# Low parts of the weights by accumulating transfers, and unread matmuls in the first gather

## The chip, the cores and the metric

The kernel runs on one core of a Trainium2 chip. The metric is the device time of one execution in microseconds (us). The engines are TensorE (PE in the profile, its weight loads PEld), VectorE (DVE), ScalarE (ACT), GpSimd (POOL) and SyncE (SP). SP issues plain transfers; POOL issues gathers, scatters and, after the change, accumulating transfers, which go through one software queue (q0).

## The reference

Three layers follow one another on 3072 tokens of 384 values (8 heads of 48):

```python
for t in range(S):                       # linear attention, 768 steps, 4 x 8 heads
    cur = einsum('bhd,bhe->bhde', u[None] * kt, vt)
    y[:, :, t] = einsum('bhd,bhde->bhe', rt, state + cur)
    state = wt[:, :, :, None] * state + einsum('bhd,bhe->bhde', kt, vt)
...
expert_idx = argmax(xn @ en.T / tau)     # first layer of 8 experts: one expert per token
out[mask] = gate_w * (relu(x[mask] @ w1[e]) @ w2[e])
...
order = argsort(-logits.flatten())       # second layer: greedy, 384 tokens per expert
for idx in order: ...                    # take (token, expert) if both are still free
out[mask] = relu(x[mask] @ w1[e]) @ w2[e]
```

w1 is 384 x 1024 and w2 is 1024 x 384 for each of the 8 experts of both layers, all in float32.

## The kernel before, in words

The kernel computes float32 products from two parts of each operand. `hi` is the value rounded to the matmul's format (fp32r), `lo` is what is left, and `prod3` (L548 to L550) adds hi x hi, hi x lo and lo x hi. So every weight is split once: it lands in a tile `stage` (three buffers of 128x1536, 768 KB, half of a weight matrix), ScalarE copies it into `whi`, and the low part `wlo = stage - whi` is computed by another engine. `whi` and `wlo` have three buffers each (`wpool`).

The attention (0 to about 225 us) runs in 24 chunks. A step begins on VectorE with the scan L295. VectorE makes the scaled r, k and masked products, TensorE transposes and multiplies, ScalarE copies transposes out of PSUM (kT L322, xT L389) and makes `cv` (L341). After steps 4, 8, 12 and so on the tokens of the steps done are given to experts (`choose`) and POOL scatters them to the expert's rows (L442). Beside this the first three weight matrices of the first expert layer are loaded (`early`, by `wparts`), their low part on POOL (L196); from the fourth step on, each step takes one piece.

The first expert layer (to about 512 us) is not touched by the change; its weights go through `wload`, low parts on VectorE.

The second expert layer (to 844 us) has eight phases, one expert each, with w1 products (`pH`), relu and split into h2h (ScalarE, L544) and h2l (VectorE, L545), and w2 products (`pY`). Which expert is next, and which 384 tokens it takes, is found by `chain(p)`: a search in which VectorE writes comparison tables (`cmp`, L972), TensorE counts with them (L983, L990, L994) and VectorE reads the counts; it gives `ei`, the expert's number. `compact` turns the chosen tokens into row numbers `ix` with one-hot matmuls (L1107, L1111), and POOL gathers the rows (L1124, three transfers of 128 rows). `tin` transposes them (pX, L1164). `load2(p, i)` fetches the two weight matrices of phase p once `ei` is known and splits them: ScalarE `whi` L1149, VectorE `wlo` L1150, in four pieces of 128x384 per half, so 16 pieces per phase. The chain, the gather and the loads of phase p+1 run during phase p. In the last two phases no search is left.

The order of the work on each engine is fixed ahead of the run by a scheduler that simulates the program with priorities; `issue_after` ties an operation behind another. Each engine then works through its list and waits at its head.

Of the kernel before, what the change touches and what calls it, by code (L numbers as in the profile page):

```python
# [26 lines left out]
DM = H * D  # L27
N = B * S
E = 8
# [15 lines left out]
WST = 3  # L45
TB = 2
# [29 lines left out]
WNQ = 2  # L76
# [7 lines left out]
def tile_kernel(ctx: ExitStack, tc, rd, kd, wd, vd, ud, emb, tau, m1w1, m1w2, m1w2t, wg2, m2w1, m2w2, out):  # L84
# [99 lines left out]
    def wparts(i, e, nq=2, eng=None):  # L184
        hi = wpool.tile([128, FW], F32R, name="whi")
        lo = wpool.tile([128, FW], F32R, name="wlo")
        WT[i, e] = (hi, lo)
        h = FW // 2
        for q in range(2):
            t = stg.tile([128, h], F32, name="stage")  # L190
            nc.sync.dma_start(t, M1[i][e][:, q * h:(q + 1) * h])
            g = h // nq
            for o in range(0, h, g):
                s = slice(q * h + o, q * h + o + g)
                nc.scalar.copy(hi[:, s], t[:, o:o + g])  # L195
                (eng or nc.vector).tensor_tensor(lo[:, s], t[:, o:o + g], hi[:, s].bitcast(F32), op=ALU.subtract)  # L196
                yield
# [45 lines left out]
    with tc.tile_pool(name="ld", bufs=3) as ld, tc.tile_pool(name="wk", bufs=2) as wk, \  # L243
# [220 lines left out]
        early = (x for i, e in ((0, 0), (1, 0), (0, 1)) for x in wparts(i, e, WNQ, nc.gpsimd))  # L464
# [6 lines left out]
        for st in range(NST):  # L471
# [23 lines left out]
            if st > WST:  # L495
                next(early, None)
# [417 lines left out]
    with tc.tile_pool(name="m2", bufs=2) as mp, tc.tile_pool(name="ps2", bufs=2, space=PSUM) as ps:  # L914
# [9 lines left out]
        oqi = [None]  # L924
        pcm = ps.tile([128, 512], F32, name="pcm", bufs=1)

        def chain(p):
# [4 lines left out]
            if not last:  # L932
# [30 lines left out]
                for s in range(3):  # L963
                    for lv in range(2):
# [17 lines left out]
                        for a in range(J // 2):  # L982
                            nc.tensor.matmul(px, cmp[:, 2 * KS * a:2 * KS * a + 128],  # L983
                                             oh[:, 2 * a:2 * a + 2, :].rearrange("p b e -> p (b e)"),
                                             start=(a == 0), stop=(a == J // 2 - 1))
                        xs = small([128, 2, E], "xs", FP16)
                        nc.vector.tensor_tensor(xs, px.rearrange("p (b e) -> p b e", b=2), par16, op=ALU.mult)
                        pa = pcn[:, o:o + 8]
                        for b in range(2):
                            nc.tensor.matmul(pa[:, :E], psum2, xs[:, b], start=(b == 0), stop=(b == 1))  # L990
# [3 lines left out]
                        nc.tensor.matmul(pb[:, :E], ones[:KS, :], fl, start=True, stop=True)  # L994
# [134 lines left out]
        def load2(p, i):  # L1129
# [7 lines left out]
            for q in range(2):  # L1137
# [7 lines left out]
                pieces = LP0 if p == 0 else LP  # L1145
                g = h // len(pieces)
                for r, e in enumerate(pieces):
                    c = slice(q * h + r * g, q * h + r * g + g)
                    nc.scalar.copy(hi[:, c], t[:, r * g:r * g + g])  # L1149
                    (nc.vector if e == "v" else nc.gpsimd).tensor_tensor(lo[:, c], t[:, r * g:r * g + g], hi[:, c].bitcast(F32),  # L1150
                                                                         op=ALU.subtract)
# [126 lines left out]
```

## Time and profile before

| | |
|---|---|
| Median of 3 runs | 845.6 us (840.58 to 848.67) |
| Profiled execution | 846.28 us, span 844.4 us, mean granted TensorE clock 0.933 |
| Busy share of the span | PE 91%, DVE 66%, ACT 40%, POOL 20% |
| PE in the chain that ended last | 53% of the span |
| q1 (plain transfers) | 87.71 MB, 32.0% of the 16 DMA engines' span |
| q0 (POOL's transfers) | 18.98 MB, 6.3% |

A line of the trace names an instruction by its line in the kernel, its engine, the operation and the tiles it writes and reads. "Idle before" is the time its engine stood still before it, with what ended that. A granted clock of 1.00 is TensorE's level of 2.4 GHz, 0.5 would be the level of 1.2 GHz all the time. Shares of busy time are averages over stages with different limits, so the stages are read apart.

### The profile page before, as it was taken

How to read it: one execution, taken by the hardware profiler on the slowest of the kernel's cores; microseconds unless marked ns; L12 is line 12 of the kernel's file. 1: busy time of each engine (PE TensorE's matmuls, PEld its weight loads, DVE VectorE, ACT ScalarE, POOL GpSimd, SP SyncE). 2: the span in 40 equal slices, each digit the busy share in tenths (PEclk: the TensorE clock that was granted, in tenths of full speed). 3: DMA queues.
4: the chain of work that ended last, by engine and by line, in shares of the span. 5: the costliest groups of instructions: out<-in, count | busy, mean ns of one | idle time of the engine just before them, and what ended most of it. 6: DMA issues, size and time to landing. Idle time of an engine off the chain costs nothing.

```text
span 844.4 us, 14670 instructions
## 1 busy us (share of the span) xinstructions
PE 771.9 (91%) x5373; PEld 675.0 (80%) x5373; DVE 556.1 (66%) x1719; ACT 335.5 (40%) x851; POOL 168.0 (20%) x173
## 2 busy tenths in 40 slices
PE   5998979999889998899999999697979889899997
PEld 4877768888389897898989888485868778789997
DVE  9998999998425435333644556676878788786430
ACT  3544645556324444334543411333323323335431
POOL 3014540121200320303032002302021221222011
PEclk9997889999979999999999999797969879899999
DMA  8775664540343353333433002332323243426300
GB/s 279 232 247 198 227 219 147 179 142 19 126 144 114 127 167 112 110 106 105 152 123 105 5 1 103 133 111 77 132 75 133 80 155 94 150 68 235 110 29 29
DMA packets 39302, 107.64 MB, mean 127 GB/s; under 512 B 6667, under 2 KB 16701, under 8 KB 39229
## 3 DMA queue, kind: packets, MB, share of 16 engines
q1 hardware_dynamic: 32060, 87.71, 32.0%
q0 software_dynamic: 7168, 18.98, 6.3%
q8 instruction: 43, 0.70, 0.4%
q14 instruction: 31, 0.25, 0.1%
HBM read 87.16 MB, written 19.90 MB: 127 GB/s over the span
## 4 chain that ended last, share of the span: by engine, by line
PE 53%; issue 9%; DVE 4%; POOL 2%; another core or an unknown queue 1%; ACT 1%; DMA 1%; ACTq 0%; POOLq 0%; DVEq 0%
PE pH L548 8%; PE pY L550 7%; PE pY L548 7%; PE pH L549 7%; PE pH L550 7%; PE pY L549 7%; PE pO L687 2%; PE pX L654 2%; PE pcm L1111 1%; PE pcn L983 1%; DVE wlo L1150 1%; POOL x L1124 1%; POOL out_dram L1193 1%; PE pX L1164 1%
## 5 line engine op out<-in xcount | busy, mean ns | idle before, releaser
L548 PE MATMUL pH<-xhi,whi 128*128 128x416 f32 x192 | 73.8, 385 | 11.7 <-DVE hl L545 7.5
L545 DVE SCALAR_TENSOR_TENSOR hl<-pH,hh 128x416 fp32r<-128x416 f32 x64 | 37.6, 590 | 70.6 <-ACT hh L544 60.2
L1150 DVE TENSOR_TENSOR wlo<-stage,whi 128x384 fp32r<-128x384 f32 x128 | 68.3, 550 | 7.0 <-ACT whi L1149 6.8
L548 PE MATMUL pH<-x2h,whi 128*128 128x384 f32 x192 | 70.9, 370 | 1.8 <-DVE h2l L545 1.6
L549 PE MATMUL pH<-x2l,whi 128*128 128x384 f32 x192 | 70.8, 369 | 0.0
L1149 ACT CAST whi<-stage 128x384 fp32r<-128x384 f32 x128 | 57.1, 511 | 33.8 <-PE pH L549 20.2
L550 PE MATMUL pH<-xhi,wlo 128*128 128x416 f32 x192 | 70.3, 367 | 0.0
L549 PE MATMUL pH<-xlo,whi 128*128 128x416 f32 x192 | 70.2, 366 | 0.0
L550 PE MATMUL pH<-x2h,wlo 128*128 128x384 f32 x192 | 69.7, 363 | 0.0
L544 ACT ACTIVATE h2h<-pH 128x384 fp32r<-128x384 f32 x64 | 31.4, 491 | 91.8 <-PE pH L550 90.8
L550 PE MATMUL pY<-whi,h2l 128*128 128x384 f32 x192 | 67.6, 355 | 0.0
L548 PE MATMUL pY<-whi,h2h 128*128 128x384 f32 x192 | 67.4, 351 | 0.0
L549 PE MATMUL pY<-wlo,h2h 128*128 128x384 f32 x192 | 66.8, 349 | 0.0
L195 ACT CAST whi<-stage 128x512 fp32r<-128x512 f32 (+1 forms) x90 | 51.7, 647 | 33.6 <-PE pY L549 23.0
L196 DVE TENSOR_TENSOR wlo<-stage,whi 128x512 fp32r<-128x512 f32 x78 | 48.3, 686 | 25.1 <-ACT whi L195 25.1
L550 PE MATMUL pY<-hh,wlo 128*128 128x416 f32 x168 | 60.4, 360 | 0.0
L548 PE MATMUL pY<-hh,whi 128*128 128x416 f32 x168 | 60.1, 358 | 0.0
L764 POOL DMA_INDIRECT lg<-lr,ids x24 | 23.1, 961 | 185.9 <-DVE lr L689 180.7
L549 PE MATMUL pY<-hl,whi 128*128 128x416 f32 x168 | 59.1, 352 | 0.0
L544 ACT ACTIVATE hh<-pH 128x416 fp32r<-128x416 f32 x64 | 32.8, 515 | 62.5 <-PE pH L550 48.5
L362 PE MATMUL y<-vv,am 128*128 128x48 f32 x384 | 56.3, 276 | 0.0
L1193 POOL DMA_INDIRECT out_dram<-orow,ix x24 | 24.4, 1015 | 156.4 <-ACT orow L1192 141.7
(327 smaller groups left out, 1904.7 us busy)
## 6 DMA issues: line engine op xcount, KB each, us to landing
stage<-in_m1w_dram SPq DMA_DIRECT2D x32, 768.0 KB
stage<-in_m2w_dram SPq DMA_DIRECT2D x32, 768.0 KB
wz<-in_w_dram SPq DMA_DIRECT2D x24, 260.0 KB
rd<-in_r_dram SPq DMA_DIRECT2D x24, 256.0 KB
kd<-in_k_dram SPq DMA_DIRECT2D x24, 256.0 KB
xg<-zt SPq DMA_DIRECT2D x8, 627.2 KB
xr<-xg SPq DMA_DIRECT2D x24, 193.0 KB
vv<-in_v_dram SPq DMA_DIRECT2D x24, 192.0 KB
```

The source lines that it names most:

```text
L195: nc.scalar.copy(hi[:, s], t[:, o:o + g])
L196: (eng or nc.vector).tensor_tensor(lo[:, s], t[:, o:o + g], hi[:, s].bitcast(F32), op=ALU.subtract)
L362: yi = nc.tensor.matmul(y[:, o:o + D], ams[h][:, p, :], vv[:, 2 * p + h, :], start=(c == 0), stop=(c == 0 or h == 1))
L544: nc.scalar.activation(hi, pH, AF.Relu)
L545: nc.vector.scalar_tensor_tensor(lo, pH, 0.0, hi.bitcast(F32), op0=ALU.max, op1=ALU.subtract)
L548: nc.tensor.matmul(o, wh, xh, start=start, stop=False)
L549: nc.tensor.matmul(o, wh, xl, start=False, stop=False)
L550: pe[0] = nc.tensor.matmul(o, wl, xh, start=False, stop=stop)
L764: s = nc.gpsimd.indirect_dma_start(out=dst, out_offset=bass.IndirectOffsetOnAxis(ap=d["ids"][:m, a:a + 1], axis=0), in_=src, in_offset=Non ...
L1149: nc.scalar.copy(hi[:, c], t[:, r * g:r * g + g])
L1150: (nc.vector if e == "v" else nc.gpsimd).tensor_tensor(lo[:, c], t[:, r * g:r * g + g], hi[:, c].bitcast(F32), op=ALU.subtract)
L1193: s_ = nc.gpsimd.indirect_dma_start(out=out, out_offset=bass.IndirectOffsetOnAxis(ap=d["ix"][:, a:a + 1], axis=0), in_=orow, in_offset=None)
```

## The change

- `ADD` names phases 1 to 5 of the second expert layer. For their weights ScalarE writes `whi` and then `-hi` into `wlo` (a scaled copy of the stage into the rounded format), piece by piece; when a half is done, POOL issues one transfer of 768 KB from `stage` that is added to `wlo` in place. The VectorE subtract stays for phases 0, 6 and 7.
- The early weights of the first layer take the same way, in pieces of 128x384 (`WNQ` 4 in place of 2, two pieces per step), in place of the subtract on POOL.
- `warm` adds 42 matmuls of 128x384 with bf16 operands into a `pY` tile that nobody reads, behind the matmuls of the first rounds of `chain(1)`; `HW` has their numbers.

```diff
--- before.py
+++ after.py
@@ -43,6 +43,8 @@
 FP16 = mybir.dt.float16
 SPLIT = 4096.0
 WST = 3
+HW = ((2, 6), (2, 24), (8,))
+ADD = (1, 2, 3, 4, 5)
 TB = 2
 LP0 = "vvvv"
 LP = "vvvv"
@@ -73,7 +75,7 @@
 IT = 1
 OQ = 4
 NSC = 2
-WNQ = 2
+WNQ = 4
 GROUPS = (4, 4, 4, 4, 4, 2, 1, 1)
 GS = max(GROUPS)
 HA = 2
@@ -181,7 +183,7 @@
     M1 = (m1w1, m1w2)
     FW = KT * FF
 
-    def wparts(i, e, nq=2, eng=None):
+    def wparts(i, e, nq=2, add=False):
         hi = wpool.tile([128, FW], F32R, name="whi")
         lo = wpool.tile([128, FW], F32R, name="wlo")
         WT[i, e] = (hi, lo)
@@ -193,7 +195,12 @@
             for o in range(0, h, g):
                 s = slice(q * h + o, q * h + o + g)
                 nc.scalar.copy(hi[:, s], t[:, o:o + g])
-                (eng or nc.vector).tensor_tensor(lo[:, s], t[:, o:o + g], hi[:, s].bitcast(F32), op=ALU.subtract)
+                if add:
+                    nc.scalar.activation(lo[:, s], t[:, o:o + g], AF.Copy, scale=-1.0)
+                    if o + g == h:
+                        nc.gpsimd.dma_start(lo[:, q * h:(q + 1) * h], t.bitcast(F32R), accum_op=ALU.add)
+                else:
+                    nc.vector.tensor_tensor(lo[:, s], t[:, o:o + g], hi[:, s].bitcast(F32), op=ALU.subtract)
                 yield
 
     def wload(i, e, nq=WQ):
@@ -461,7 +468,7 @@
         s2(1)
         s3(0)
         route_consts()
-        early = (x for i, e in ((0, 0), (1, 0), (0, 1)) for x in wparts(i, e, WNQ, nc.gpsimd))
+        early = (x for i, e in ((0, 0), (1, 0), (0, 1)) for x in wparts(i, e, WNQ, True))
         ends, chosen, slot_of = {}, [], {}
         for n in GROUPS:
             s0 = len(slot_of)
@@ -493,7 +500,8 @@
                 if st > 1 and tables:
                     table()
             if st > WST:
-                next(early, None)
+                for _ in range(2):
+                    next(early, None)
             if st == WF:
                 wfold(E - DEF)
             if st > E:
@@ -922,6 +930,14 @@
 
         plan = {}
         oqi = [None]
+        hq = []
+
+        def warm(i, n):
+            if not hq:
+                hq.append(ps.tile([128, DM], F32, name="pY"))
+            with tc.issue_after(i.ins):
+                for _ in range(n):
+                    nc.tensor.matmul(hq[0], ones, ioq.rearrange("p s j -> p (s j)")[:, :DM], start=True, stop=True)
         pcm = ps.tile([128, 512], F32, name="pcm", bufs=1)
 
         def chain(p):
@@ -980,18 +996,24 @@
                         o = 16 * lv
                         px = pcn[:, 48 + o:64 + o]
                         for a in range(J // 2):
-                            nc.tensor.matmul(px, cmp[:, 2 * KS * a:2 * KS * a + 128],
+                            wi = nc.tensor.matmul(px, cmp[:, 2 * KS * a:2 * KS * a + 128],
                                              oh[:, 2 * a:2 * a + 2, :].rearrange("p b e -> p (b e)"),
                                              start=(a == 0), stop=(a == J // 2 - 1))
+                        if p == 1 and s == 1 and lv == 0:
+                            warm(wi, HW[2][0])
                         xs = small([128, 2, E], "xs", FP16)
                         nc.vector.tensor_tensor(xs, px.rearrange("p (b e) -> p b e", b=2), par16, op=ALU.mult)
                         pa = pcn[:, o:o + 8]
                         for b in range(2):
-                            nc.tensor.matmul(pa[:, :E], psum2, xs[:, b], start=(b == 0), stop=(b == 1))
+                            wi = nc.tensor.matmul(pa[:, :E], psum2, xs[:, b], start=(b == 0), stop=(b == 1))
+                        if p == 1 and s == 0:
+                            warm(wi, HW[lv][0])
                         fl = small([KS, E], "fl", BF16)
                         nc.vector.tensor_tensor(fl, pa[:KS, :E], need[:KS], op=ALU.is_ge)
                         pb = pcn[:, o + 8:o + 16]
-                        nc.tensor.matmul(pb[:, :E], ones[:KS, :], fl, start=True, stop=True)
+                        wi = nc.tensor.matmul(pb[:, :E], ones[:KS, :], fl, start=True, stop=True)
+                        if p == 1 and s == 0:
+                            warm(wi, HW[lv][1])
                         nn = small([128, 1], "nn", bufs=4)
                         nc.vector.reduce_max(nn, pb[:, :E], axis=AX.X)
                         if lv == 0:
@@ -1143,12 +1165,17 @@
                                       mybir.DependencyInfo(mybir.DependencyClass.Sync, mybir.DependencyReason.DATA),
                                       reason="rows before weights")
                 pieces = LP0 if p == 0 else LP
+                add = p in ADD
                 g = h // len(pieces)
                 for r, e in enumerate(pieces):
                     c = slice(q * h + r * g, q * h + r * g + g)
                     nc.scalar.copy(hi[:, c], t[:, r * g:r * g + g])
-                    (nc.vector if e == "v" else nc.gpsimd).tensor_tensor(lo[:, c], t[:, r * g:r * g + g], hi[:, c].bitcast(F32),
-                                                                         op=ALU.subtract)
+                    if add:
+                        nc.scalar.activation(lo[:, c], t[:, r * g:r * g + g], AF.Copy, scale=-1.0)
+                    else:
+                        nc.vector.tensor_tensor(lo[:, c], t[:, r * g:r * g + g], hi[:, c].bitcast(F32), op=ALU.subtract)
+                if add:
+                    nc.gpsimd.dma_start(lo[:, sl], t.bitcast(F32R), accum_op=ALU.add)
             d["w", i] = (hi, lo)
 
         sc_o = []
```

The order on the engines moves at more than the places of the diff. Line numbers below are those of each kernel: L1150 before is L1176 after, L1149 is L1172, L545 is L553, L1107 is L1129, L1116 is L1138, L972 is L988, L1124 is L1146, L1193 is L1220.

VectorE in the second phase (p = 1), behind the one-hot tables of the next phase's tokens, before the change:

```order
L1107 TENSOR_TENSOR oq<-ioq,pb_6925 128x128x6
L992 TENSOR_TENSOR fl<-pcn,need 46x8
L1150 TENSOR_TENSOR wlo<-stage,whi 128x384
L996 TENSOR_REDUCE nn<-pcn 128x1
L1114 COPY cp<-pcm 128x15
L1005 TENSOR_SCALAR t_7317<-nn,t_7293 128x1
L1116 SCALAR_TENSOR_TENSOR ix<-cp 128x3
L1118 TENSOR_REDUCE gg<-cp 128x3
L1007 TENSOR_SCALAR wc<-big,t_7317 128x24
L1150 TENSOR_TENSOR wlo<-stage,whi 128x384
L1009 TENSOR_SCALAR w<-wc 128x24
```

and with it:

```order
L1129 TENSOR_TENSOR oq<-ioq,pb_7002 128x128x6
L1012 TENSOR_TENSOR fl<-pcn,need 46x8
L1018 TENSOR_REDUCE nn<-pcn 128x1
L1136 COPY cp<-pcm 128x15
L1027 TENSOR_SCALAR t_7398<-nn,t_7374 128x1
L1138 SCALAR_TENSOR_TENSOR ix<-cp 128x3
L1140 TENSOR_REDUCE gg<-cp 128x3
L1029 TENSOR_SCALAR wc<-big,t_7398 128x24
L553 SCALAR_TENSOR_TENSOR h2l<-pH,h2h 128x384
L1031 TENSOR_SCALAR w<-wc 128x24
```

The subtracts between the steps of the search are gone, and h2l stands where one of them stood.

ScalarE in the first phase (p = 0), at its last relu, before the change:

```order
L540 CAST x2h<-pX 128x384 x3
L544 ACTIVATE h2h<-pH 128x384 x8
L1149 CAST whi<-stage 128x384 x12
L1192 ACTIVATE orow<-pY,gg 128x384
L540 CAST x2h<-pX 128x384 x2
```

and with it, with the tiles' numbers (the w1 halves of p = 1 are stage_6522 and stage_6533, h2h_6596 is the eighth relu of p = 0):

```order
L552 ACTIVATE h2h_6582<-pH_6572 128x384
L1172 CAST whi_6520<-stage_6522 128x384
L1174 ACTIVATE wlo_6521<-stage_6522 128x384
...
L1172 CAST whi_6520<-stage_6533 128x384
L1174 ACTIVATE wlo_6521<-stage_6533 128x384
...
L552 ACTIVATE h2h_6596<-pH_6586 128x384
```

Eight copies and eight negated copies now stand between the seventh and the eighth relu; before, all eight relus came first.

POOL from the first phase's scatters to the gather of p = 2 (x_6966 before, x_7043 after), before the change:

```order
L1124 DMA x_6008<-y_67,ix 128x384 x3
L1124 DMA x_6406<-y_67,ix 128x384 x3
L1193 DMA out_dram<-orow,ix 3072x384 x3
L1124 DMA x_6966<-y_67,ix 128x384 x3
L1193 DMA out_dram<-orow,ix 3072x384 x3
```

and with it:

```order
L1178 DMA wlo<-stage 128x1536
L1146 DMA x_6479<-y_67,ix 128x384 x3
L1178 DMA wlo<-stage 128x1536
L1220 DMA out_dram<-orow,ix 3072x384
L1178 DMA wlo<-stage 128x1536
L1220 DMA out_dram<-orow,ix 3072x384
L1178 DMA wlo<-stage 128x1536
L1220 DMA out_dram<-orow,ix 3072x384
L1178 DMA wlo<-stage 128x1536 x2
L1146 DMA x_7043<-y_67,ix 128x384 x3
```

Each gather but the first has one or two accumulating transfers right ahead of it in POOL's list and on the same queue.

## Rows read from the trace of the kernel before

**Rows 1.** Windows of the attention: length, busy us (and count) per engine, PEclk, DMA share, GB/s.

```profile
45.90:122.60 76.70, 66.21 (x535) 55.88 (x531) 69.60 (x129) 39.07 (x123) 32.86 (x20) 0.80 0.65 216
122.60:196.80 74.20, 72.49 (x712) 61.59 (x714) 73.58 (x173) 39.68 (x143) 8.47 (x8) 1.00 0.48 148
```

**Rows 2.** Timeline of DVE, L295 (start us, us, operation, count).

```profile
45.86 1.23 DVE L295 TENSOR_TENSOR_SCAN PI<-wz,ind 128x516 f32<-128x516 f32 x1
...
122.62 1.22 DVE L295 TENSOR_TENSOR_SCAN PI<-wz,ind 128x516 f32<-128x516 f32 x1
...
196.81 1.23 DVE L295 TENSOR_TENSOR_SCAN PI<-wz,ind 128x516 f32<-128x516 f32 x1
```

**Rows 3.** Groups of DVE, 50 to 125 us: busy us, mean ns, idle before and releasers.

```profile
L310 DVE SCALAR_TENSOR_TENSOR z<-rd,ut,kd 128x128 f32<-128x128 f32 x27 | 19.5, 736 | 0.0
```

**Rows 4.** The same group of DVE, 130 to 205 us.

```profile
L310 DVE SCALAR_TENSOR_TENSOR z<-rd,ut,kd 128x128 f32<-128x128 f32 x40 | 13.1, 337 | 0.0
```

**Rows 5.** Waits of DVE, 45 to 125 us: total us, times, longest.

```profile
DVE tm L369 <- PE KV L275: 5.0, 2, 3.8
```

**Rows 6.** Groups of POOL, 40 to 130 us.

```profile
L196 POOL TENSOR_TENSOR wlo<-stage,whi 128x768 fp32r<-128x768 f32 x12 | 23.4, 1969 | 71.9 <-ACT whi L195 71.9
```

**Rows 7.** Groups of ACT, 50 to 125 us.

```profile
L195 ACT CAST whi<-stage 128x768 fp32r<-128x768 f32 x11 | 8.7, 829 | 1.6 <-DMA stage<-in_m1w_dram 1.6
```

**Rows 8.** A window before the early weights are split.

```profile
20.00:40.00 20.00, 20.00 (x195) 16.90 (x195) 19.67 (x48) 10.38 (x38) 0.00 (x0) 1.00 0.76 230
```

**Rows 9.** Timeline of PE at the first gather (in brackets idle before, releaser).

```profile
543.03 0.66 PE L1164 MATMUL pX<-ident,x 128*128 128x128 f32 x2 [4.53 <-DMA x<-y,ix]
545.31 0.48 PE L1164 MATMUL pX<-ident,x 128*128 128x128 f32 x1 [1.62 <-DMA x<-y,ix]
...
549.66 0.52 PE L548 MATMUL pH<-x2h,whi 128*128 128x384 f32 x1
549.99 0.52 PE L549 MATMUL pH<-x2l,whi 128*128 128x384 f32 x1
```

**Rows 10.** Windows of the second expert layer's phases, columns as in Rows 1.

```profile
552.50:763.20 210.70, 189.93 (x1431) 164.94 (x1431) 163.82 (x709) 69.42 (x154) 39.38 (x33) 0.89 0.32 110
763.20:816.10 52.90, 52.90 (x308) 51.72 (x307) 27.92 (x57) 25.35 (x57) 8.94 (x9) 1.00 0.41 138
```

**Rows 11.** Groups of PE, L549: 552 to 763 us, then 763 to 816.

```profile
L549 PE MATMUL pH<-x2l,whi 128*128 128x384 f32 x120 | 46.0, 384 | 0.0
...
L549 PE MATMUL pY<-wlo,h2h 128*128 128x384 f32 x120 | 42.6, 358 | 0.0
...
L549 PE MATMUL pH<-x2l,whi 128*128 128x384 f32 x48 | 16.1, 336 | 0.0
```

**Rows 12.** Waits of PE, 540 to 845 us: total us, times, longest.

```profile
PE pX L1164 <- DMA x<-y,ix: 11.5, 4, 4.6
PE pcn L983 <- DVE cmp L972: 8.7, 4, 2.5
...
PE pH L548 <- DVE h2l L545: 1.6, 2, 1.5
```

**Rows 13.** Timelines of ACT and DVE in the second phase.

```profile
606.96 0.49 ACT L544 ACTIVATE h2h<-pH 128x384 fp32r<-128x384 f32 x1 [1.55 <-PE pH L550]
...
620.66 0.54 DVE L545 SCALAR_TENSOR_TENSOR h2l<-pH,h2h 128x384 fp32r<-128x384 f32 x1
```

**Rows 14.** Timelines of POOL and PE at the gather of the next phase.

```profile
577.28 1.09 POOL L1124 DMA_INDIRECT x<-y,ix  x1 [32.86 <-DVE gg L1118]
...
580.35 2.14 POOL L1124 DMA_INDIRECT x<-y,ix  x1 [0.30 <-issue]
...
584.57 0.69 PE L1164 MATMUL pX<-ident,x 128*128 128x128 f32 x2 [0.71 <-DMA x<-y,ix]
```

**Rows 15.** DMA, 600 to 625 us: GB/s in 40 equal slices.

```profile
GB/s 0 0 0 0 0 0 0 157 88 364 413 403 442 423 416 413 442 220 20 0 0 0 0 0 26 0 0 0 0 59 147 315 403 391 381 229 194 84 0 0
```

**Rows 16.** Groups of ACT, 552 to 763 us.

```profile
L1149 ACT CAST whi<-stage 128x384 fp32r<-128x384 f32 x83 | 37.1, 511 | 26.5 <-PE pH L549 18.4 <-DMA stage<-in_m2w_dram 7.9
```

## The prediction, made before the changed kernel ran

> **What bounds the kernel now.** I read the windows first, because the share of busy time changes from stage to stage, then the groups of instructions of one engine in one stretch, then the waits of TensorE, and last the timelines at the places the change touches.
>
> In the attention VectorE is the bound: it is busy 69.60 of 76.70 us while the early weights are split and 73.58 of 74.20 us after that [rows 1]. A step is counted from one L295 scan to the next. Seven steps take 45.86 to 122.62 us, 76.8 us; the next ten take 122.62 to 196.81, 74.2 us, or 7.42 each [rows 2]. Both stretches hold the expert choice about every fourth step, so seven steps at 7.42 would be 51.9 us: the early stretch has 24.8 us too many. They lie on VectorE itself: L310 has a mean of 736 ns against 337 later [rows 3, 4]; 27 x 0.40 is 10.8 us in this one line. L369 waits 5.0 us more, for KV from TensorE [rows 5]. The twelve POOL subtracts of 1.97 us, 23.4 us in all, are the only work of the stretch that is missing later [rows 6]: a VectorE operation that meets one lasts until it ends.
>
> In the second expert layer TensorE is the bound, but not evenly. From 552.5 to 763.2 us, five phases with a selection search beside the matmuls, it is busy 189.93 of 210.70 us at a granted clock of 0.89; from 763.2 on, phases without the search, 52.90 of 52.90 at 1.00 [rows 10]. So the five phases contain 20.8 us of idle time and slow matmuls on top: L549 has means of 384 ns (pH) and 358 (pY) there against 336 [rows 11]. Six groups of 120 weight matmuls, on average 35 ns slower, with two overlapping at any time, are 720 x 0.035 / 2, about 12 us. The waits name the releasers: 8.7 us for the comparison tables of VectorE (cmp), 1.6 for h2l, and 11.5 for the gathered rows, of which the first two of 4.5 and 1.6 belong to the first gather [rows 9, 12]. VectorE is late because its order is fixed and the low parts of the weights stand ahead: in the second phase ScalarE had h2h at 606.96, VectorE reached its h2l at 620.66 [rows 13].
>
> **Attention.** Removed: 12 POOL subtracts. With them go the stretched VectorE operations; of the 24.8 us nothing else explains more than noise, so the ceiling is 25 us. Added on ScalarE: 24 copies and 24 negated copies of 128x384 at 0.51 [rows 16] for 12 copies at 0.83 [rows 7]: 24.5 - 10.0 = 14.5 us. ScalarE was busy 39.07 of 76.70 us [rows 1], so it holds them, but they stand in its order between the copies that TensorE waits for (kT, xT, cv); about half, 7 us, I charge as delay. Added on the DMA: six accumulating transfers of 768 KB. The DMA engines were at 0.65 over 76.7 us, 49.9 us of work [rows 1]; six transfers add 11 to 58 us by the bounds below, and 49.9 + 11 is already more than 51.9. Part is prefetch that may slip, part are loads that steps need, and ScalarE waits in order for the stages. Without any early weights steps ran at a share of 0.76 [rows 8], so there is little room. I charge 7 us more. Attention: 25 - 7 - 7 = **11 us gained**, between 0 and 22.
>
> **One accumulating transfer.** No row shows one. From below: the plain loads of the same 768 KB, with the same 6 KB per partition, run at 403 to 442 GB/s [rows 15], or 1.8 us. From above: the three gathers of one phase on the same software queue move 590 KB between the first issue at 577.28 and the last wait's end at 584.57 [rows 14], 81 GB/s, which gives 9.7 us. I take 4.5, because size and rows are those of the load, and reading the destination doubles that load's 1.8 before any start-up. The Trainium skill ("DMA: Bandwidth & Descriptors", Anatomy of one DMA) gives a software-queue transfer about 2.0 us plus its bytes at 436 GB/s, an estimate of 3.8 us here without the second read; the sum by it would be the same within 2 us.
>
> **First gather.** The 42 unread matmuls stand between the first search rounds and the transposes. TensorE was idle 4.53 us until 543.03, and afterwards weight matmuls came every 0.32 us [rows 9], where at the full clock two overlap at 0.34. Full clock over the 5.4 us to 551 would gain 2.7. At 0.17 to 0.32 each they take 7 to 13 us, in an idle stretch of 4.5 plus the 1.6 of the next wait and the gaps of the search; at the slow rate they delay the transposes by up to 5. Between -2.7 and +5 I take **1 us gained**.
>
> **Phases 0 to 4 of the second layer.** 80 VectorE subtracts go (phases 1 to 5 are loaded during phases 0 to 4). That removes the waits for cmp and h2l, 10.3 us, and the slow clock that follows them: of the waits in these phases, 10.3 for VectorE stand beside 5.4 for gathered rows (11.5 less 6.1), so about two thirds of the 12 us, 8. Together 18. ScalarE gets 80 negated copies, 41 us over 210.7 where it is busy 69.42 [rows 10]. In phases 0 and 1 the order sets sixteen split operations in one block of 8 us ahead of an h2h; TensorE has up to two finished products and the search in hand, some 5 us, so I charge 2.5 us twice. The gathers stand behind adds on POOL; in phase 2 they were issued well before use, so I charge nothing: the cover is the rest of the compute phase, and without it an add's 4.5 us show whole. Sum: **13 us gained**, between 3 and 20.
>
> The Trainium skill ("DMA: Bandwidth & Descriptors", SWDGE vs HWDGE vs iDMA) says that GpSimd writes the descriptors of its transfers into SBUF and that VectorE's two-port modes lock it out meanwhile. The rows allow it: a gather's issue took 1.09 us once and 2.14 another time beside VectorE work [rows 14].
>
> **Sum.** 11 + 1 + 13 = 25 us off the profiled 846.3 (span 844.4 and 1.9 around it), 821; that run is 0.7 above the median of the three, so **820 us**. The likeliest case's own range is 806 to 834.
>
> **Rivals.**
> *ScalarE becomes what VectorE was* (0.16). It takes every split piece in a fixed order. For: blocks of sixteen ahead of an h2h. Against: its share stays near 55%. If each block costs its 8 us less 2 in all five phases, with the clock after it, the phases gain nothing and the attention about 10: 836.
> *The attention goes over to the DMA engines* (0.13). By the 9.7 us price 58 us of adds meet 49.9 of loads; even at 4.5 it is 77, the old length. Then the attention gains nothing, the rest 14: 831.
> *The software queue is the bound: slower* (0.11). Per phase four adds, three gathers and three scatters share it. At 9.7 us that is 38.8 + 7.3 + 3 = 49 us against 42.1 per phase now (210.7 / 5): 35 us lost over five phases, 10 kept elsewhere, 870. It decides from (42.1 - 10.3) / 4 = 8 us per add. For: the gathers' 81 GB/s. Against: their rows are 1.5 KB, these 6 KB.
> *POOL is held by VectorE* (0.05). Each add issued 1.1 us later (2.14 less 1.09), gathers behind them: 5 x 1.1 and the clock after it, 827. This is the rule on descriptors named above.
> *More than forecast* (0.07). All of the stretch and all waits gone: 25 + 2.7 + 18, 800.
> *It does nothing* (0.05), both engines merely trading waits: 845.
>
> **Chances and range.** The forecast has 0.43. About 1%, 8.5 us, is what a measurement of this kernel tells from no change. Faster by more: the forecast, most of the first two rivals, the fourth and fifth, 0.78. Within it: 0.10, the sixth and the bad ends of the first two. Slower: 0.12. The range 799 to 843 leaves out the slower case, the sixth, and little else.
>
> **What would show it.** In the trace after: a mean of L310 under 400 ns and steps near 8 us from 46 us on (attention); cmp waits of TensorE under 3 us in all (phases); matmuls at full rate right after the first gather; an accumulating transfer near 4.5 us in the software queue's rows. It is wrong if TensorE waits long for h2h or for gathered rows, or if VectorE waits in the attention for operands that the DMA brings late.

## The result, and the profile after

The changed kernel took 816.9 us (813.5 to 820.9, four runs), the kernel before 846.4 beside it: a ratio of 0.966 with an interval of 0.959 to 0.973. The prediction was 820 with a range of 799 to 843. Beside each other again on another chip, where the kernel before took 826.8, the change took 798.9, a ratio of 0.963 (0.954 to 0.972). That chip and a third one give the first expert layer another length (341 us from the last attention step to the first `ix` on the chip of the two profiles shown here, 321 to 324 on the second, 342 to 345 on the third with that layer unchanged); so runs are compared by ratios and by stages, not by bare times. The trace of the second comparison is of its slowest execution, 804.2 us, where the other three took 789.9 to 799.2; its ratio is that of those three.

The two profiled executions by stage, from the starts of rows (L295 of VectorE becomes L302, L544 of ScalarE L552, L1116 L1138):

| Stage | before | after | difference |
|---|---|---|---|
| Start to the attention step at 46 us | 45.9 | 46.0 | +0.2 |
| To the last attention step | 150.9 | 140.7 | -10.3 |
| To the first `ix` of the second expert layer | 340.6 | 340.7 | +0.1 |
| To the first relu of phase 0 | 15.0 | 13.5 | -1.5 |
| Phases 0 to 4 (to the first relu of phase 5) | 210.7 | 189.6 | -21.1 |
| Rest | 81.2 | 82.6 | +1.4 |
| Span | 844.4 | 813.2 | -31.2 |

The windows of the profile after, with the columns of [rows 1]: the early steps of the attention, the five phases with a search, and two without.

```profile
45.90:111.00 65.10, 60.76 (x531) 50.40 (x528) 52.61 (x129) 43.82 (x143) 12.77 (x11) 0.87 0.88 263
...
541.00:730.60 189.60, 180.05 (x1433) 154.04 (x1432) 130.78 (x628) 101.50 (x234) 54.05 (x53) 0.99 0.79 209
730.60:783.40 52.80, 52.80 (x307) 51.56 (x306) 26.23 (x53) 25.50 (x59) 9.13 (x10) 1.00 0.36 124
```

The phases answer to [rows 10]: TensorE stood 9.6 us idle where it was 20.8, and its granted clock is 0.99 for 0.89. The DMA share went from 0.32 to 0.79.

The waits of TensorE from 500 us on, in the columns of [rows 12]: total, times, longest.

```profile
PE pX L1191 <- DMA x<-y,ix: 6.1, 4, 3.6
PE pcn L999 <- DVE oh L978: 1.5, 1, 1.5
...
PE pcn L999 <- DVE cmp L988: 0.5, 1, 0.5
```

cmp fell from 8.7 us to 0.5, h2l is no longer in the list. What stays is the gathered rows: the 6.1 us of the first gather [rows 9] are gone, behind unread matmuls, but in the five phases the wait for rows did not shrink, 6.1 us for the 5.3 of before.

VectorE's groups and its waits in the early steps, for [rows 3 and 5], and the steps at their end, for [rows 2]:

```profile
L317 DVE SCALAR_TENSOR_TENSOR z<-rd,ut,kd 128x128 f32<-128x128 f32 x28 | 9.3, 347 | 0.0
...
L302 DVE TENSOR_TENSOR_SCAN PI<-wz,ind 128x516 f32<-128x516 f32 x7 | 8.7, 1236 | 0.0
```

```profile
DVE sel L439 <- PE y L437: 6.7, 2, 4.3
DVE tm L376 <- PE KV L282: 3.9, 2, 2.1
DVE mx L417 <- ACT LG L415: 1.9, 2, 1.2
```

```profile
111.14 1.24 DVE L302 TENSOR_TENSOR_SCAN PI<-wz,ind 128x516 f32<-128x516 f32 x1
...
186.72 1.24 DVE L302 TENSOR_TENSOR_SCAN PI<-wz,ind 128x516 f32<-128x516 f32 x1
```

L310 of before, L317 now, is back at 347 ns. But VectorE now waits 10.6 us for products of TensorE (`y`, `KV`) and 1.9 for ScalarE; before it waited 5.0 for `KV` [rows 5] and 2.0 for `y`. Seven steps from 46.0 to 111.1 us still take 65.1, 9.3 each, not the 52 of undisturbed ones; TensorE is busy 60.8 of 65.1 us at a clock of 0.87.

The software queue's rows of the two pages, before and after, with packets, MB and their share of 16 engines' span:

```profile
q0 software_dynamic: 7168, 18.98, 6.3%
```

```profile
q0 software_dynamic: 10912, 39.43, 19.6%
```

6.3% of 844.4 us is 53 us, 19.6% of 813.2 is 159: if the gathers and scatters keep their 53, the 26 transfers take 106 us of all 16 engines together, 4.1 each. The first one of the phases shows the same alone. POOL issues it at 558.12; in the GB/s from 555 to 570 us, in slices of 0.375 us, its bytes move from 559.1 to about 563.2:

```profile
558.12 0.98 POOL L1178 DMA_DIRECT2D wlo<-stage  x1 [24.75 <-ACT wlo L1174]
```

```profile
GB/s 459 426 410 377 197 55 16 0 0 0 0 44 246 197 82 246 246 262 131 147 262 246 17 16 0 0 160 176 344 107 131 295 279 410 438 328 373 397 262 213
```

That is 5.1 us from POOL's issue to the last byte. Beside other transfers it is longer: the trace of the second execution of this kernel has the time from issue to landing, here as a median of 26, with the size:

```profile
wlo<-stage POOLq DMA_DIRECT2D x26, 768.0 KB, 7.6
```

TensorE around the first gather, for [rows 9]: the last unread matmuls end at 536, the transposes follow, and weight matmuls come every 0.17 us, not 0.32, from the first on.

```profile
530.45 4.09 PE L940 MATMUL pY<-ioq,ones 128*128 128x384 bf16 x24
...
536.03 0.52 PE L1191 MATMUL pX<-ident,x 128*128 128x128 f32 x3
...
539.09 0.34 PE L558 MATMUL pH<-x2h,wlo 128*128 128x384 f32 x1
539.26 0.34 PE L556 MATMUL pH<-x2h,whi 128*128 128x384 f32 x1
```

### The profile page after: what moved, and what is told of

The parts are those of the page before. It is cut to its first block, busy times and chain, and to the rows that moved or that the text cites. A ratio compares the mean times of both kernels' runs of the same rounds, so it can differ in the third digit from the quotient of the medians.

```text
span 813.2 us, 14843 instructions
## 1 busy us (share of the span) xinstructions
PE 763.3 (94%) x5415; PEld 660.6 (81%) x5415; DVE 505.0 (62%) x1639; ACT 377.4 (46%) x967; POOL 168.1 (21%) x187
## 3 DMA queue, kind: packets, MB, share of 16 engines
q0 software_dynamic: 10912, 39.43, 19.6%
## 4 chain that ended last, share of the span: by engine, by line
PE 44%; issue 18%; DMA 3%; POOL 3%; DVE 2%; another core or an unknown queue 1%; ACT 1%; POOLq 0%; ACTq 0%
PE pY L556 6%; PE pY L558 6%; PE pY L557 6%; PE pH L558 5%; PE pH L556 5%; PE pH L557 5%; DMA x<-y,ix 3%; PE pO L695 2%; PE pcm L1133 2%; PE pcn L999 1%; POOL out_dram L1220 1%; PE pY L940 1%; PE pX L662 1%; PE pX L1191 1%
## 5 line engine op out<-in xcount | busy, mean ns | idle before, releaser
L553 DVE SCALAR_TENSOR_TENSOR hl<-pH,hh 128x416 fp32r<-128x416 f32 x64 | 37.5, 590 | 66.9 <-ACT hh L552 54.7
L1172 ACT CAST whi<-stage 128x384 fp32r<-128x384 f32 x128 | 61.7, 509 | 21.9 <-DMA stage<-in_m2w_dram 11.8
L197 ACT CAST whi<-stage 128x512 fp32r<-128x512 f32 (+1 forms) x102 | 54.4, 593 | 33.3 <-PE pY L557 23.0
L556 PE MATMUL pH<-x2h,whi 128*128 128x384 f32 x192 | 66.4, 347 | 0.3
L558 PE MATMUL pH<-x2h,wlo 128*128 128x384 f32 x192 | 66.7, 348 | 0.0
L557 PE MATMUL pH<-x2l,whi 128*128 128x384 f32 x192 | 66.1, 345 | 0.0
L552 ACT ACTIVATE h2h<-pH 128x384 fp32r<-128x384 f32 x64 | 31.3, 490 | 60.7 <-PE pH L558 48.2
L552 ACT ACTIVATE hh<-pH 128x416 fp32r<-128x416 f32 x64 | 32.5, 514 | 57.7 <-PE pH L558 49.6
L556 PEld LDWEIGHTS pH<-xhi,whi 128*128 128x128 f32 x192 | 38.2, 200 | 16.8 <-DVE hl L553 10.8
L348 ACT ACTIVATE cv<-vv,cs 128x48 f32<-128x48 f32 x192 | 46.2, 325 | 11.0 <-DVE cs L345 10.4
```

The costliest lines, as they stand in the source:

```text
L348: nc.scalar.activation(cv[:, h], d["v"][:, h], AF.Copy, scale=cs[:, h:h + 1])
L552: nc.scalar.activation(hi, pH, AF.Relu)
L553: nc.vector.scalar_tensor_tensor(lo, pH, 0.0, hi.bitcast(F32), op0=ALU.max, op1=ALU.subtract)
L556: nc.tensor.matmul(o, wh, xh, start=start, stop=False)
L557: nc.tensor.matmul(o, wh, xl, start=False, stop=False)
L558: pe[0] = nc.tensor.matmul(o, wl, xh, start=False, stop=stop)
```

## The experiments

In all of them the stage lengths are read as in the table. The first four ran on the second chip, beside a kernel before of 827.1 us.

**The attention alone.** `ADD` is empty and no unread matmul is issued.

```diff
-HW = ((2, 6), (2, 24), (8,))
-ADD = (1, 2, 3, 4, 5)
+HW = ((0, 0), (0, 0), (0,))
+ADD = ()
```

> Only the early weights of the attention get their low parts by accumulating transfers; phases and first gather as before. Theory (stretched VectorE operations vanish, ScalarE and the DMA engines give part back): last attention step about 10 us earlier, whole time 10 us under the kernel before (about 836). Rival (the attention's gain is given back before the first expert layer starts, because weights are late): 0 to 3 us. Rival (the full 25 us is there and only hidden by the rest of the change): 820.

Measured: 824.2 us, ratio 0.998 (0.995 to 1.001). The last step began at 192.8 us, 3.5 and 3.9 earlier than the 196.3 and 196.7 of the two kernels below that keep the POOL subtracts. TensorE's wait for cmp is where it was:

```profile
PE pcn L1001 <- DVE cmp L990: 8.7, 4, 2.4
```

The theory's 10 us did not come, nor did the second rival's 820. The 2.8 us lie in the range of the first rival, but its reason does not show: from the last step to the first `ix` this kernel takes 323.4 us, the next two 322.4 and 323.4. And the interval holds 1, so the gain in the whole time is not clear of noise. By its steps the attention is worth less in this execution than in the first pair, 4 us and not 10: from 46 us to the last step this kernel takes 146.8 us, the next two, with POOL subtracts, 150.4 and 150.8, where the first pair had 140.7 and 150.9.

**The phases alone.** `wparts` and its call as before the change, `HW` zero.

```diff
-        early = (... for x in wparts(i, e, WNQ, True))      # WNQ 4, two pieces per step
+        early = (... for x in wparts(i, e, WNQ, nc.gpsimd)) # WNQ 2, one piece per step
-HW = ((2, 6), (2, 24), (8,))
+HW = ((0, 0), (0, 0), (0,))
```

> Only phases 1 to 5 of the second expert layer change; POOL subtracts stay in the attention, no unread matmuls. Theory (VectorE waits of TensorE and the slow clock behind them vanish): 19 to 21 us under the kernel before, about 826; TensorE's waits for cmp under 1 us, clock of the five phases 0.97 or more. Rival (much of the phases' 21 us in the complete change comes from the unread matmuls starting the phases at the full clock): 13 to 15 us. Rival (ScalarE blocks cost 5 us): 13 us.

Measured: 816.1 us, ratio 0.985 (0.975 to 0.994), 11 us. Windows of the five phases and of phase 5:

```profile
534.10:728.40 194.30, 183.35 (x1412) 158.21 (x1412) 128.85 (x623) 101.99 (x235) 49.79 (x50) 0.95 0.75 198
728.40:758.20 29.80, 28.24 (x175) 26.57 (x174) 16.44 (x38) 12.86 (x31) 9.09 (x9) 1.00 0.62 210
```

The five phases last 194.3 us where the attention-only kernel has 210.9 on this chip: 16.6 gained. But phase 5 takes 29.8 us, 3.3 more than in it; part of the one-hot matmuls of the last tokens stands there now, with a wait. So the phases give 16.6, more than the 13 predicted, and the order gives 3 back. No wait for cmp is left in the five phases, as the theory had it, but its 19 to 21 us did not come, and the clock is 0.95, not 0.97: 11 us are nearer to the rivals' 13. The largest wait of TensorE in the five phases is now for gathered rows, 7.7 us, where the kernel before had 5.3:

```profile
PE pX L1187 <- DMA x<-y,ix: 7.7, 3, 3.0
```

**The unread matmuls alone.** `ADD` empty, `wparts` as before.

> Only the 42 unread matmuls are added. Theory: transposes of the first gather start about 3 us later, matmuls after it at the full clock: 1 to 2 us gained. Rival (the clock does nothing, the delay stays): 3 to 7 us slower. Rival (the phase after it also keeps the full clock): 5 us gained.

Measured: 822.2 us, ratio 0.995 (0.992 to 0.997), 5 us faster. First `ix` to first relu is 13.5 us for 15.4 without them: 1.9 at the place itself. From the first `ix` to the end it is 302.0 for 307.5: 5.5. The rest is 5.2 us in the five phases, 205.7 for 210.9 at a clock of 0.92 for 0.89, less 1.6 lost in phase 5. The wait for cmp stays TensorE's largest, with 6.1 us in three waits:

```profile
PE pcn L993 <- DVE cmp L982: 6.1, 3, 2.1
```

The time is that of the last rival, in which the phase behind also keeps the full clock. But the added instructions also give the scheduler another order for the later phases; how much of the 3.6 is order and how much clock, this run can't tell.

**The change without them.** Only `HW` is zero.

> The complete change without the 42 unread matmuls. Theory: 1 to 2 us slower than the complete change, about 818, 28 to 30 under the kernel before. Rival (the phases need the full clock at their start): 823 to 825. Rival (they only delay the transposes): 813.

Measured: 814.4 us, over runs from 801 to 818, too wide for a ratio. The profiled one takes 294.4 from the first `ix`, where the complete change takes 285.7 on the first chip and 286.5 on this one. Against the first it is 1.6 before the first relu, 3.5 in the five phases, 3.6 in phase 5. The rival that the phases need the unread matmuls is nearer than my 1 to 2 us. That they need them for the clock is not shown: the five phases run at 0.96 here, at 0.97 to 0.99 in two executions of the complete change, and the order differs too.

The next four ran on the second chip again, beside a kernel before of 826.8.

**The complete change again.** No edit.

> The complete change once more, beside the kernel before on the chip of this call, since the four kernels of the first call met another chip, on which the kernel before took 827. Theory (sum of parts read from the traces so far: attention 4 to 10, first gather and phases 21): 27 to 30 us under the kernel before on any chip. Rival (parts of the first comparison belong to the chip): 13 to 18 us, as the complete change without the unread matmuls gave (12.7).

Measured: 798.9 us, 27.9 under the kernel before, ratio 0.963 (0.954 to 0.972). The theory holds for the sum. The parts alone gave 2.8, 11.0 and 4.9 us, 18.7 in all. That they are worth more together is not shown: the intervals of the ratios put the whole between 23 and 38 us, and the three parts together between about 10 and 28. In the traces the parts add up. From the first `ix` to the end it is 307.5 us with neither, 12.5 less with the new splits, 5.5 less with the unread matmuls, 18.2 less with both (the next run), and 21.0 less here; the steps of the attention give 2 to 6. Where the gain lies does change: phase 5 takes 29.8 and 30.1 us with the new splits alone, and 26.4 to 26.5 where the unread matmuls are there too.

**The change with POOL subtracts in the attention.** `wparts` and its call as before.

> The complete change with the early weights of the attention left on POOL as before. Theory (the unread matmuls and the phases belong together: first gather to end took 285.7 us in the complete change, 295.0 with the phases alone, 302.0 with the unread matmuls alone, 307 with neither): 21 us from the first gather to the end gained, 5 to 10 slower than the complete change by the attention. Rival (the attention's earlier end is waited away in the first expert layer): the same time as the complete change.

Measured: 805.3 us, ratio 0.972 (0.965 to 0.980); 6.4 us more than the complete change. By the traces it takes 150.3 us from 46 us to the last step, where five kernels with the new attention, one of them without its transfers, took 145.2 to 148.5 on this chip, and 289.3 behind the first `ix`, where the complete change takes 285.7 and 286.5. The theory holds for the attention; behind the first `ix` 18 us are gained, not 21. The intervals of this kernel and the complete one overlap, so the rival isn't shut out by the times alone.

**No transfers in the attention.**

```diff
-                    if o + g == h:
+                    if False:
                         nc.gpsimd.dma_start(lo[:, q * h:(q + 1) * h], t.bitcast(F32R), accum_op=ALU.add)
```

> The complete change with the six accumulating transfers of the attention left out (the low parts of three matrices stay at -hi); ScalarE's work and everything else stay. Theory (the DMA engines limit the early steps, 0.87 to 1.02 busy): the steps from 46 to 111 us shorten by 4 to 8 us. Rival (ScalarE's pieces are what is left): under 2 us.

Measured: 806.2 us over two runs, ratio 0.975 (0.967 to 0.984); the last step begins at 194.3, in the complete change on this chip at 194.5, in the kernel with the new attention alone, which has the transfers too, at 192.8. Windows of the early steps, this kernel first, then that one on the same chip:

```profile
45.90:80.00 34.10, 30.86 (x249) 25.84 (x246) 27.60 (x66) 20.88 (x70) 5.52 (x4) 0.80 0.69 223
80.00:111.00 31.00, 29.95 (x242) 24.92 (x242) 20.49 (x53) 20.21 (x68) 0.50 (x1) 0.78 0.63 219
```

```profile
45.90:80.00 34.10, 30.87 (x264) 25.85 (x260) 28.62 (x68) 21.59 (x73) 4.43 (x5) 0.84 0.85 257
80.00:111.00 31.00, 29.95 (x243) 24.64 (x243) 21.01 (x54) 20.43 (x66) 5.71 (x6) 0.79 0.85 237
```

The DMA share is 0.69 and 0.63 instead of 0.85 and 0.85, and nothing got faster. TensorE is busy 29.95 of 31 us in both, at 0.78 and 0.79. The theory falls: the transfers cost the attention nothing that shows, as it stands.

**Every transfer of the phases twice.**

```diff
                 if add:
-                    nc.gpsimd.dma_start(lo[:, sl], t.bitcast(F32R), accum_op=ALU.add)
+                    for _ in range(2):
+                        nc.gpsimd.dma_start(lo[:, sl], t.bitcast(F32R), accum_op=ALU.add)
```

> Every accumulating transfer of the phases is issued twice (the low parts come out wrong), all else as in the complete change; it prices the transfer and shows how near the software queue is to being the bound. By the trace a transfer takes 3.9 us on all 16 engines and the phases have them 0.79 busy, so 4 more per phase, 16 us in 38, can't be covered whole: the five phases 8 to 10 us longer each, 40 to 50 us in all. Rival (the queue has room, the share counts idle packets): under 10 us in all.

Measured: 859.0 us, ratio 1.039 (1.030 to 1.048), 60 us over the complete change. The five phases, and TensorE's waits in them:

```profile
527.70:770.30 242.60, 193.90 (x1433) 164.53 (x1432) 132.38 (x628) 100.70 (x234) 73.48 (x75) 0.88 0.92 224
```

```profile
PE pX L1192 <- DVE x2l L549: 17.3, 3, 10.1
PE pH L558 <- DMA wlo<-stage: 8.1, 1, 8.1
PE pcn L1014 <- DVE fl L1012: 7.4, 2, 7.1
```

53 us longer than the 189.6 of the complete change for 20 more transfers, 2.7 each. That is not the price of the transfers alone: POOL stands 15 times until an earlier transfer has landed, and with it the gathers and scatters behind in its order. In the five phases of the complete change none of its waits is for a transfer.

```profile
POOL wlo L1179 <- DMA wlo<-stage: 84.8, 15, 10.6
```

This is near the prediction's slower rival, made to happen: with 8.2 us of transfers for each half instead of 4.1 the DMA engines are 0.92 busy, and the kernel is slower than before. The rival put the turning point at 8 us; on a straight line from 189.6 us of phases at 4.1 to 242.6 at 8.2, the old 210.7 is reached at 5.7, an estimate with POOL's waits in it.

The next three ran on the third chip, beside a kernel before of 847.5.

**No negated copies in the attention.** POOL sets the low parts to zero instead.

```diff
-                    nc.scalar.activation(lo[:, s], t[:, o:o + g], AF.Copy, scale=-1.0)
+                    if o == 0:
+                        nc.gpsimd.memset(lo[:, q * h:(q + 1) * h].bitcast(F32), 0.0)
```

> The complete change, but ScalarE's 24 negated copies of the attention are left out; POOL sets the low parts to zero early instead (they come out as the whole weight). Leaving out the six transfers moved the steps by nothing, so two explanations stay for the 15 us that the seven early steps still have over 52. Theory (ScalarE's pieces delay the copies that TensorE waits for, and TensorE falls to the low clock): without the 24 copies, 12.6 us of ScalarE, the last step starts at 187 or earlier instead of 194. Rival (TensorE's low clock comes from elsewhere in these steps): the last step stays within 2 us of 194.

Measured: 828.5 us over two runs, ratio 0.979 (0.973 to 0.985). The last step began at 193.3; by the letter that is the rival's sign. But the second step began at 16.1 for 9.6, since the zeroing stands in the start-up, so lengths count. From the seventh step on it took 140.6 us, and the next six steps 47.6, where eight executions with the negated copies, two pieces to a step, took 57.0 to 62.4. Stages that landed sooner beside a later start do not explain this: in none of the eight does ScalarE wait for a stage in these steps. Windows of those six steps, this kernel first (with the window behind them), then the kernel with the new attention alone, on the second chip:

```profile
52.70:100.30 47.60, 45.87 (x458) 39.05 (x454) 44.96 (x112) 30.39 (x104) 9.89 (x8) 1.00 1.00 304
100.30:116.00 15.70, 8.14 (x53) 6.76 (x51) 7.64 (x19) 7.07 (x22) 5.70 (x6) 0.61 1.03 300
```

```profile
46.00:106.70 60.70, 56.42 (x457) 46.58 (x454) 45.23 (x113) 39.08 (x130) 8.03 (x8) 0.80 0.83 246
```

TensorE has the full clock, and VectorE is busy nearly throughout again, 44.96 of 47.60 us, as TensorE is; a step takes 7.9 us. Then one wait takes 8 us back, with the DMA engines full (1.03) while the six transfers run in a row:

```profile
DVE tm L377 <- PE KV L283: 8.1, 1, 8.1
```

So the negated copies on ScalarE held the early steps, and TensorE's low clock came with them, as far as one execution shows it; the DMA engines are the next limit behind. The whole kernel gained nothing by it: its ratio is 0.979, where the complete change has 0.963 and 0.966 on other chips.

**Negated copies of the phases twice.**

```diff
                     if add:
-                        nc.scalar.activation(lo[:, c], t[:, r * g:r * g + g], AF.Copy, scale=-1.0)
+                        for _ in range(2):
+                            nc.scalar.activation(lo[:, c], t[:, r * g:r * g + g], AF.Copy, scale=-1.0)
```

> Each of ScalarE's 80 negated copies in the phases is made twice (same values), all else as in the complete change: 8 us more ScalarE per phase on 20 of 38. Theory (ScalarE is not near its limit, its blocks cost nothing now): under 8 us in all. Rival of the prediction (ScalarE becomes what VectorE was): 4 to 8 us per phase, 20 to 40 in all.

Measured: 839.4 us, ratio 0.991 (0.987 to 0.995), where the complete change has 0.963. In the trace the first `ix` to the end takes 300.8 us for 285.7. Windows of the five phases and phase 5:

```profile
554.40:751.90 197.50, 184.78 (x1439) 158.02 (x1438) 131.24 (x627) 131.87 (x311) 54.42 (x54) 0.97 0.74 193
751.90:785.50 33.60, 28.73 (x146) 27.84 (x147) 13.99 (x29) 14.30 (x34) 5.35 (x6) 0.90 0.64 197
```

8 us more in the five phases and 7 more in phase 5, for 30 us more of ScalarE's busy time in the five (131.87 for 101.50; the 8 us per phase of the expectation are too many, since its copies start 0.41 us apart). By the traces that is between theory and rival; by the ratios, 0.991 for 0.963 and 0.966, it is 21 to 24 us, in the rival's range. ScalarE has room for the change, not for twice of it.

**The first expert layer's weights as well.**

```diff
     def wload(i, e, nq=WQ):
-        for _ in wparts(i, e, nq):
+        for _ in wparts(i, e, nq, True):
```

> The complete change, and the rest of the first expert layer's weights (78 subtracts of VectorE, 48 us) by accumulating transfers too. Theory (TensorE is busy 98 to 100% of that layer on the chip of these runs, so freeing VectorE gains nothing, and scatters queue behind transfers): the same as the complete change or 2 to 5 us slower. Rival (VectorE's waits there, 7.5 us for hl on the first chip, are the subtracts'): 5 to 15 us faster than the complete change.

Measured: 843.3 us, ratio 0.995 (0.991 to 1.000): the gain of the change is nearly gone. That layer takes 356.9 us for 342 to 345 on this chip, with waits of TensorE for ScalarE's yT that the kernel before doesn't have:

```profile
PE pO L695 <- ACT yT L688: 8.0, 6, 1.9
PE pH L556 <- DVE hl L553: 6.8, 6, 2.7
```

Worse than the theory's 2 to 5, in the same direction. The rival falls: the wait for hl is 6.8 us without any subtract of VectorE in that layer.

**One piece per attention step.** On a fourth chip, beside a kernel before of 823.6.

```diff
-                for _ in range(2):
-                    next(early, None)
+                next(early, None)
```

> The complete change with one piece of the early weights per attention step in place of two: the same 48 operations of ScalarE, spread over some two steps more, though one step still holds 15. Leaving 24 of them out let TensorE keep the full clock up to 80 us and took 8 to 10 us off the early steps. Theory (it is how many pieces stand ahead of a copy that TensorE waits for): last step 2 to 5 us earlier than in the complete change on the same stretch (46 us to the last step: 148.4 in the second execution of it, 140.7 in the first), 2 to 5 us faster in all. Rival (the number of pieces counts, not where they stand): no difference.

Measured: 810.8 us, ratio 0.983 (0.977 to 0.989): slower than the complete change. The seven early steps ended at 109.4, in other kernels with the new attention at 110.5 to 115.7; but the last began at 203.7. The later pieces reached ScalarE's order ahead of their stage. Rows of ScalarE, then of VectorE:

```profile
124.95 0.51 ACT L197 CAST whi<-stage 128x384 fp32r<-128x384 f32 x1 [5.42 <-DMA stage<-in_m1w_dram]
```

```profile
131.23 0.19 DVE L417 TENSOR_REDUCE mx<-y 128x4 f32<-128x32 f32 x1 [4.88 <-ACT LG L415]
...
143.57 0.19 DVE L439 TENSOR_TENSOR sel<-y,oh 128x32 f32<-128x32 f32 x1 [5.18 <-PE y L437]
```

ScalarE stood 5.4 us for a stage, and VectorE twice 5 us for what came after it. The theory of places isn't settled by this; the edit made another wait. No version here beats the complete change, though the interval of the one with POOL subtracts in the attention overlaps with its own.

## Why the prediction was right

**The sum.** Forecast 25 us, measured 29.5 between the medians and 31.2 between the profiles: the likeliest case, in its own range of 806 to 834. The cause in the phases was right and its size too small. On the second chip, where the gain was 27.9, the sum owes something to luck: by the traces the attention gave 2 to 6 us of its 11 there, and the phases more than their 13. Of the signs named, L317's mean, cmp, the matmuls behind the first gather and the time on the software queue came as said. Steps near 8 us did not come, they took 9.3; that sign did not fit the sum either, since 76.8 less 11 us is 9.4 a step.

**The attention, 11 us.** 10.3 on the first chip, by its steps; 2 to 6 in the traces of the second. The cause was right: L317 has 347 ns. The ceiling of 25 was reached by no run: even without the negated copies six steps took 7.9 us each, not 7.4, and a wait behind them gave 8 us back. Of what comes off, the part for ScalarE (7) was too small and the part for the DMA engines (7) was wrong: without the transfers the steps didn't move, without the negated copies they went to 7.9 us. That both together, 14, meet the 13.2 that the first pair lacks (65.1 less 51.9) is luck. What I had not in the sum is how ScalarE's copies cost: TensorE runs part of these steps at the 1.2 GHz level (0.79 to 0.84 in the windows), is then itself busy nearly all the time, and VectorE waits for it. [rows 1] had that clock, 0.80 for the early stretch.

**The transfer, 4.5 us.** 4.1 by the queue's share, as time on the engines. As a time from issue to landing, the way the phases' term uses it, 4.5 was too short: 5.1 alone and 7.6 as a median. The formula of the Trainium skill ("DMA: Bandwidth & Descriptors", Anatomy of one DMA) gave an estimate of 3.8, about 2.0 of it fixed; the trace does not agree, since the bytes alone move for 4.1 us. Its rule on VectorE holding up GpSimd's descriptors (same page, SWDGE vs HWDGE vs iDMA) shows in no row here: the issue of a transfer took 0.94 us on average and 1.02 at most, that of a gather 1.05 on average. The rival *POOL is held by VectorE* had each issue 1.1 us later. POOL's groups of the five phases:

```profile
L1146 POOL DMA_INDIRECT x<-y,ix x20 | 20.9, 1046 | 18.1 <-DVE wc L1029 6.1 <-DVE gg L1140 4.1 <-issue 4.0
L1178 POOL DMA_DIRECT2D wlo<-stage x20 | 18.8, 939 | 94.9 <-ACT wlo L1174 82.8 <-PE pcn L999 12.1
```

**The first gather, 1 us.** 1.5 in the first pair, 1.9 alone. The 42 matmuls are worth more than that, 5 us alone by the median, through later phases: as far as they change the scheduler's order that is no property of the gather, and it wasn't in the prediction. The first gather's wait for rows is gone, but the matmuls that fill it take most of its time.

**The phases, 13 us.** 21.1 in the first pair, 16.6 alone; this term was mis-sized. The charge for ScalarE's blocks, 5 us, was not paid. The block is there in phase 0, but its sixteen operations start 0.41 us apart, not 0.51, so it takes 6.6 us and not 8:

```profile
554.01 0.49 ACT L552 ACTIVATE h2h<-pH 128x384 fp32r<-128x384 f32 x1 [1.07 <-PE pH L558]
554.39 0.50 ACT L1172 CAST whi<-stage 128x384 fp32r<-128x384 f32 x1
554.80 0.53 ACT L1174 ACTIVATE wlo<-stage 128x384 fp32r<-128x384 f32 x1
...
560.61 0.53 ACT L1174 ACTIVATE wlo<-stage 128x384 fp32r<-128x384 f32 x1
561.04 0.47 ACT L552 ACTIVATE h2h<-pH 128x384 fp32r<-128x384 f32 x1
```

yet no wait for h2h stands among TensorE's waits: the search's and the one-hot matmuls and the finished products covered it. And I left a third of the slow clock in place for the gathers; in the first pair the clock came back to 0.99, though the gathers still wait 6.1 us. With the new splits alone it came back to 0.95 only. For the gathers behind adds I charged nothing; their wait in the five phases went from 5.3 us to 6.1, and to 7.7 with the new splits alone.

**The rivals.** The slower one was real at twice the transfers, with 60 us, and its turning point of 8 us per transfer was too high, since at 8.2 the five phases were already 32 us longer than before; at 4.1 it leaves the phases a DMA share of 0.79. ScalarE as what holds the others is real in the attention, though it is busy only 43.8 of 65.1 us there, and in the phases begins with twice the negated copies. That the attention goes over to the DMA engines is refuted as it stands, and comes behind ScalarE.

## What to carry to other kernels

When work moves from one engine to two others, price each by its limit in the stage where it lands: here a phase of 38 us had room for one transfer of 4.1 us per half weight, and none for two. An engine that was never the bound, ScalarE, still decided the attention; that it does so because its copies stand between TensorE's operations in a fixed order is argued, not shown. And an edit in a scheduled program moves work far from its place: unread matmuls at the first gather took 3.4 to 3.6 us off phase 5 when the new splits were there, and added 1.6 when they were not.

## What the runs showed that was not expected

The accumulating transfer of 768 KB takes 4.1 us on all 16 engines, about twice the 1.8 of the plain load [rows 15]. Its `stage` is free only when it has landed: in the five phases SyncE waits 83.3 us in ten waits for such transfers before it issues the next load. The attention with the new splits took 140.7 us from 46 us on on one chip and 145.2 to 148.5 on another, at clocks of 0.84 and, with the new attention alone, 0.79 from 80 to 111 us. The last seven steps take 51.3 us in the first execution of the complete change and in the second; the three before them take 24.3 at a clock of 1.00 in the first and 28.4 at 0.88 in the second. The unchanged first expert layer took 341 us on one chip and 321 to 324 on another; why stays open.
